# Loading the v tile of an attention unit with one transfer instead of three

## The chip, the cores and the metric

The kernel runs on one core of one Trainium2 chip. The metric is the device time of one execution in microseconds (us). The core has five engines that run their own instruction queues side by side: TensorE (PE; its weight loads are shown apart, as PEld), VectorE (DVE), ScalarE (ACT), GpSimd (POOL) and SyncE (SP). In this kernel SP does no arithmetic; it issues nearly all transfers between HBM and the on-chip memory, in program order, and stops at the first one whose wait isn't met. 16 DMA engines move the data.

## The reference

Linear attention with two softmaxes, and then a token-and-channel mixer on its output. In float32, with batch 8, 8 heads, 576 positions and head size 64:

```python
q_s = softmax(q, axis=-1)                      # over the 64 features
k_s = softmax(k, axis=2)                       # over the 576 positions
kv  = einsum('bhsd,bhse->bhde', k_s, v)        # 64 x 64 per head
x   = einsum('bhsd,bhde->bhse', q_s, kv)       # then laid out as (8, 576, 512)

h   = relu(x.T @ w_tok1) @ w_tok2              # over positions: 576 -> 256 -> 576
u   = x + h.T
out = u + relu(u @ w_ch1) @ w_ch2              # over channels: 512 -> 1536 -> 512
```

## The kernel before

The attention and the token mixing run unit by unit. A unit is one batch and two heads (128 features); there are 32 units, n = 0 to 31. Positions go on the 128 partitions: 576 positions make C = 4 full blocks of 128 and a tail of TL = 64, so that a tile has C1 = 5 blocks. The host lays out the input arrays with that padding; rows 64 to 127 of the tail block repeat the last 64 positions. The matmuls that make `kv` (`stage_kv`, L355) multiply all 5 blocks over all 128 partitions, so what those repeated rows hold must count for nothing there: in the v tile they are zero.

The v tile `v_t` is `[128, 5 blocks, 2 heads, 65]`. Columns 0 to 63 hold v, and column 64 holds ones, which makes the softmax's sum come out of the same matmul. `v_tile` (L60) allocates it once and lets POOL set the ones (L62) and then the whole tail rows, ones column included, to zero (L63). `load_v` (L180) then writes v into the 64-wide parts around the ones column, with three transfers: the 4 full blocks of head 0, those of head 1 (both L184), and the 64 rows of the tail for both heads (L185). As 65 columns lie between one head's part and the next, each contiguous run that the transfer writes is 64 floats, 256 bytes.

The first 8 units (the early ones) use two v tiles in turn, the other 24 units one. `load_v(n + 1)` (or `n + 2` for early units) is issued behind the matmuls of `stage_kv(n)`, and its transfer waits until the last unit in that buffer has been read by them. On the SP queue the v transfers stand between others: `kt_t` (L169) and `q_t` (L161), `k_t` (L174, late units alone), the weight loads `stg` and `stg_w` (L196, L222), the loads and stores that keep sums of weights in HBM (L502, L503, L511, L519), and from 300 us on the `ring` loads (L546), 252 blocks of weights that the channel mixing uses up one after the other.

The early units (until about 80 us) come with the widening and splitting of the weights on DVE and ACT. After that the list `steps` goes over 9 groups of 512 positions and 12 blocks of the hidden channels: `ch1` (L482), or `pair_a` and `pair_b` with `product` (L593), and `ch2` (L642). The late units are put between these steps by the table `todo`. The order on each engine is then set when the program is built, by a planner that simulates the times of all instructions, transfers included:

```python
with tile.TileContext(nc, schedule_with_timeline_sim=True) as tc:
    attn_mixer_kernel(tc, *args, out, dims)
```

Of the kernel before, what the change touches and what calls it, by code (L numbers as in the profile page):

```python
# [15 lines left out]
P = 128  # L16
# [4 lines left out]
def attn_mixer_kernel(ctx: ExitStack, tc: tile.TileContext, q, k, kt, v, wt, out, dims):  # L21
# [3 lines left out]
    nc = tc.nc  # L25
    B, H, S, D, TOK, DM, DCH, wide = dims
# [3 lines left out]
    C = S // P  # L30
    C1 = C + 1
    S0 = C * P
    TL = S - S0
# [26 lines left out]
    def v_tile(pool):  # L60
        t = pool.tile([P, C1, 2, D + 1], F32, name="v_t")
        nc.gpsimd.memset(t[:, :, :, D : D + 1], 1.0)  # L62
        nc.gpsimd.memset(t[TL:P, C, :, :], 0.0)  # L63
        return t

    v_ring = [v_tile(const)]

    ones = const.tile([P, P], F32, name="ones")
# [111 lines left out]
    def load_v(n):  # L180
        if n < NU and n not in v_of:
            t = v_ring[n % 2 if n < NE else 0]
            for h in range(2):
                nc.sync.dma_start(t[:, 0:C, h, 0:D], v[n][:, 0:C, h * D : (h + 1) * D])  # L184
            nc.sync.dma_start(t[0:TL, C, :, 0:D], v[n][0:TL, C, :].rearrange("p (h d) -> p h d", h=2))  # L185
            v_of[n] = t

    def load_weights(i, n=CW, out=None):
# [159 lines left out]
    def stage_kv(u):  # L348
        kx, vt = u["k"], v_of[u["n"]]
        kv = ps_unit()  # L350

        for c in range(C1):
            for h in range(2):
                hs = slice(h * D, (h + 1) * D)
                nc.tensor.matmul(kv[hs, 0 : D + 1], kx[:, c, hs], vt[:, c, h, :], start=(c == 0), stop=(c == C))  # L355

        if u["n"] != NE - 1:
            load_v(u["n"] + 2 if u["n"] < NE else u["n"] + 1)
        rs = sm.tile([P, 1], F32, name="rs")
        nc.vector.tensor_scalar(rs, kv[:, D : D + 1], 1e-9, None, op0=ALU.add)  # L360
        nc.vector.reciprocal(rs, rs)
        kvf = kv_ring[u["n"] % len(kv_ring)]
        for h in range(2):
            hs = slice(h * D, (h + 1) * D)
            nc.scalar.activation(kvf[hs, hs], kv[hs, 0:D], AF.Copy, scale=rs[hs])
        u["kvf"] = kvf
        if u["early"]:
            return
        kvh = wk.tile([P, P], F32R, name="kvh")
        kvl = wk.tile([P, P], F32R, name="kvl")  # L370
        split(kvh, kvl, kvf, nc.vector)
        u["kvh"], u["kvl"] = kvh, kvl
# [176 lines left out]
    rows = {}  # L549
# [161 lines left out]
    w1f = early1.tile([P, C1, TOK], F32, name="w1f")  # L711
    w1t = early1.tile([P, TOK], F32, name="w1t")
    v_ring.append(v_tile(early1))
    kv_ring += [kv_tile(early1, i) for i in range(1, NB)]

# [8 lines left out]
    load_tok1()  # L724
    first = []
    load_v(0)
    begin(1)
    stages[0][0]()
    soft(1)
    stages[0][1]()  # L730
    load_v(1)
    load_tok2()
    conv[:] = [(stg, cv)]
# [168 lines left out]
```

## Time and profile before

| what | value |
|---|---|
| time, median of 3 runs (range) | 813.62 us (811.61 to 817.54) |
| the profiled execution, its own time | 814.48 us |
| its span, first to last instruction | 812.6 us |
| mean granted TensorE clock | 0.998 |
| busy: PE, PEld, DVE, ACT, POOL | 96%, 85%, 74%, 47%, 14% of the span |
| transfers: bytes, mean rate | 147.07 MB, 181 GB/s |

The profile's page gives the busy time of each engine, a strip of 40 slices of the span, the DMA queues, the chain of work that ended last, and groups of instructions by line. A busy PE isn't a PE at its peak, because its matmuls overlap. SPq stands for the queue of SP, PEldq for that of the weight loads; issuing and waiting there aren't counted as busy time of an engine. Further views used below are the table by stretches of time, the waits (who waited for whom), the list of one tile's instructions, and the timeline of one engine.

### The profile page before, as it was taken

What the parts mean: (1) busy time and instruction counts of PE and PEld (TensorE: products, weight loads), DVE (VectorE), ACT (ScalarE), POOL (GpSimd) and SP (SyncE); (2) the same over time, 40 slices, a digit from 0 to 9 for tenths busy, and PEclk for the clock granted to TensorE, in tenths of its full rate; (3) what the DMA queues carried; (4) which work ended last, traced back from release to release, by engine and by line L of the source; (5) the groups of instructions that cost most, each with busy time, mean ns of one, the idle gap of its engine ahead of it and who ended that gap; (6) DMA issues with size and microseconds to landing.
All of it is one profiled execution on the core that took longest, in us unless ns stands there. A gap on an engine that the chain in (4) does not pass through costs nothing.

```text
span 812.6 us, 14046 instructions
## 1 busy us (share of the span) xinstructions
PE 782.8 (96%) x5112; PEld 690.4 (85%) x5112; DVE 605.3 (74%) x1195; ACT 379.9 (47%) x908; POOL 113.8 (14%) x88
## 2 busy tenths in 40 slices
PE   3899999979999999999999999999999999999998
PEld 3688888768878888899999999879999999999996
DVE  7988998789869765987798688877896546436433
ACT  4775533366555654555564455355665522112110
POOL 1000010101212151122212222122122200200000
PEclk9999999999999999999999999999999999999999
DMA  9644632425678643575667656756566445556651
GB/s 300 197 158 146 245 143 92 150 72 188 200 232 283 210 115 98 177 253 175 193 193 243 188 181 186 229 175 191 165 182 209 145 143 179 191 177 205 209 169 52
DMA packets 110852, 147.07 MB, mean 181 GB/s; under 512 B 45760, under 2 KB 57664, under 8 KB 110784
## 3 DMA queue, kind: packets, MB, share of 16 engines
q1 hardware_dynamic: 104448, 134.12, 53.3%
q10 hardware_dynamic: 6336, 12.06, 4.1%
q8 instruction: 41, 0.67, 0.3%
q14 instruction: 27, 0.22, 0.1%
HBM read 122.55 MB, written 23.59 MB: 180 GB/s over the span
## 4 chain that ended last, share of the span: by engine, by line
PE 75%; DVE 11%; DMA 7%; ACT 4%; issue 2%; SPq 1%; POOL 0%; DVEq 0%; ACTq 0%; POOLq 0%
PE ps_o L642 31%; PE ps_h L593 20%; PE ps_h L482 8%; PE ps_h L459 6%; PE ps_h L417 4%; DMA q_t<-in_q 4%; PE ps_h L355 2%; DMA stg<-in_w 1%; ACT q_t L403 1%; PE ps_h L425 1%; DVE q_t L325 1%; DVE q_t L338 1%; PE ps_h L314 1%; DMA k_t<-in_k 1%; DVE st L324 1%
## 5 line engine op out<-in xcount | busy, mean ns | idle before, releaser
L642 PE MATMUL ps_o<-h,c2h 128*128 128x512 f32 x672 | 226.0, 398 | 3.7 <-ACT h L485 3.4
L642 PEld LDWEIGHTS ps_o<-h,c2h 128*128 128x128 f32 x672 | 125.9, 189 | 29.3 <-ACT h L485 4.3
L642 PE MATMUL ps_o<-h,c2l 128*128 128x512 f32 x336 | 132.3, 395 | 0.0
L593 PE MATMUL ps_h<-th,ring 128*128 128x256 f32 x576 | 107.1, 283 | 1.3 <-DVE c L624 1.3
L593 PEld LDWEIGHTS ps_h<-th,ring 128*128 128x128 f32 x576 | 89.7, 191 | 1.5 <-DVE c L624 1.5
L593 PE MATMUL ps_h<-uh,ring 128*128 128x256 f32 x432 | 81.9, 283 | 0.5 <-ACT dg L315 0.5
L593 PE MATMUL ps_h<-tl,ring 128*128 128x256 f32 x288 | 81.4, 283 | 0.0
L593 PEld LDWEIGHTS ps_h<-uh,ring 128*128 128x128 f32 x432 | 70.3, 190 | 5.1 <-ACT dg L315 0.9
L403 ACT COPY q_t<-cv_s 32x160 f32<-32x160 f32 (+1 forms) x232 | 71.9, 310 | 2.8
L316 POOL TENSOR_TENSOR k_t<-k_t,dg 128x640 f32<-128x640 f32 x24 | 40.9, 1704 | 230.5 <-ACT dg L315 215.9
L642 PEld LDWEIGHTS ps_o<-h,c2l 128*128 128x128 f32 x336 | 63.9, 190 | 10.5
L131 POOL TENSOR_TENSOR ql<-q_t,qh 128x640 fp32r<-128x640 f32 x24 | 40.4, 1683 | 182.3 <-ACT qh L130 126.0
L593 PE MATMUL ps_h<-ul,ring 128*128 128x256 f32 x216 | 61.0, 282 | 0.0
L629 ACT ACTIVATE h<-c 128x512 fp32r<-128x512 f32 x48 | 28.9, 625 | 60.2 <-DVE c L624 60.1
L482 PE MATMUL ps_h<-uh,c1h 128*128 128x512 f32 x144 | 56.0, 391 | 0.4 <-ACT c1h L130 0.4
L482 PE MATMUL ps_h<-uh,c1l 128*128 128x512 f32 x144 | 56.2, 390 | 0.0
L482 PE MATMUL ps_h<-ul,c1h 128*128 128x512 f32 x144 | 56.1, 390 | 0.0
L593 PEld LDWEIGHTS ps_h<-tl,ring 128*128 128x128 f32 x288 | 55.2, 192 | 0.0
L466 ACT CAST uh<-ps_h 128x320 fp32r<-128x320 f32 (+4 forms) x76 | 24.8, 336 | 55.7 <-PE ps_h L459 36.5
L334 ACT ACTIVATE q_t<-q_t 128x640 f32<-128x640 f32 x32 | 23.7, 740 | 50.2 <-DVE q_t L325 34.8
L324 DVE TENSOR_REDUCE st<-q_t 128x10 f32<-128x640 f32 x32 | 26.1, 815 | 27.2 <-DMA q_t<-in_q 27.0
L403 DVE COPY q_t<-cv_s 32x160 f32<-32x160 f32 (+1 forms) x152 | 36.7, 241 | 6.8 <-POOL ql L131 5.0
(196 smaller groups left out, 1762.3 us busy)
## 6 DMA issues: line engine op xcount, KB each, us to landing
ring<-w SPq DMA_DIRECT2D x252, 256.0 KB, 3.3
kt_t<-in_kt SPq DMA_DIRECT2D x32, 320.0 KB, 3.3
q_t<-in_q SPq DMA_DIRECT2D x32, 320.0 KB, 3.4
stg_w<-in_w SPq DMA_DIRECT2D x18, 512.0 KB, 6.3
v_t<-in_v SPq DMA_DIRECT2D x64, 128.0 KB, 3.4
k_t<-in_k SPq DMA_DIRECT2D x24, 320.0 KB, 3.8
w<-stg SPq DMA_DIRECT2D x12, 512.0 KB, 3.6
stg<-in_w SPq DMA_DIRECT2D x10, 512.0 KB, 4.8
```

The source lines that it names most:

```text
L131: lo_eng.tensor_tensor(lo, src, f32(hi), op=ALU.subtract)
L316: nc.gpsimd.tensor_tensor(kx, kx, dg.unsqueeze(1).broadcast_to([P, C1, P]), op=ALU.subtract)
L324: nc.vector.tensor_reduce(st[:, 0, :], qt, axis=AX.X, op=ALU.max)
L334: nc.scalar.activation(qc, qc, AF.Exp)
L403: eng(qx[ys, 0:n, xs], turned[xs, 0:n, ys])
L417: nc.tensor.matmul(y[:, 0:TOK], a, w, start=(i == 0), stop=(i == len(mm) - 1))
L459: nc.tensor.matmul(t[:, 0:N], a, w, start=(i == 0), stop=(i == len(mm) - 1))
L466: nc.scalar.copy(uh, src).ins,
L482: nc.tensor.matmul(t, a[:, n, :], w, start=(i == 0), stop=(i == 3 * NJ - 1))
L593: nc.tensor.matmul(t[:, cols], a, b[:, n], start=(i == 0), stop=(i == 5))
L629: nc.scalar.activation(hh, c[:, r], AF.Relu)
L642: m = nc.tensor.matmul(o, a[:, cs], w, start=(first and i == 0), stop=(last and i == 2))
```

## The change

The array of v on the host gets zeros in the rows 64 to 127 of its tail block, where it repeated the last positions. `load_v` moves the whole unit, all 5 blocks, both heads and all 128 partitions, with one transfer. POOL's second memset sets only the ones column of the tail rows to zero, since the transfer now writes the rest.

```diff
@@ v_tile
         nc.gpsimd.memset(t[:, :, :, D : D + 1], 1.0)
-        nc.gpsimd.memset(t[TL:P, C, :, :], 0.0)
+        nc.gpsimd.memset(t[TL:P, C, :, D : D + 1], 0.0)
@@ load_v
             t = v_ring[n % 2 if n < NE else 0]
-            for h in range(2):
-                nc.sync.dma_start(t[:, 0:C, h, 0:D], v[n][:, 0:C, h * D : (h + 1) * D])
-            nc.sync.dma_start(t[0:TL, C, :, 0:D], v[n][0:TL, C, :].rearrange("p (h d) -> p h d", h=2))
+            nc.sync.dma_start(t.rearrange("p c h d -> p (c h) d")[:, :, 0:D], v[n].rearrange("p c (h d) -> p (c h) d", h=2))
@@ kernel, on the host
-    def rows(x):
+    def rows(x, again=None):
         x = x.reshape(nu, 2, s, d)[:, :, twice].reshape(nu, 2, c + 1, P, d)
+        if again is not None:
+            x[:, :, c, tl:] = again
...
-        "in_v": rows(inputs["v"]),
+        "in_v": rows(inputs["v"], 0.0),
```

## The prediction

> **What bounds the kernel now.** I read the page first, then the table by stretches, then the chain of waits, and last SP's timeline around v.
>
> ```profile
> span 812.6 us, 14046 instructions
> PE 782.8 (96%) x5112; PEld 690.4 (85%) x5112; DVE 605.3 (74%) x1195; ACT 379.9 (47%) x908; POOL 113.8 (14%) x88
> q1 hardware_dynamic: 104448, 134.12, 53.3%
> PE 75%; DVE 11%; DMA 7%; ACT 4%; issue 2%; SPq 1%; POOL 0%; DVEq 0%; ACTq 0%; POOLq 0%
> ...
> 0.00:20.00 20.00, 7.38 (x41) 6.04 (x42) 15.88 (x35) 9.57 (x18) 2.16 (x17) 1.00 0.97 301
> 20.00:40.00 20.00, 17.67 (x139) 13.78 (x138) 20.00 (x54) 14.58 (x33) 0.00 (x0) 1.00 0.67 198
> 60.00:80.00 20.00, 19.28 (x151) 17.18 (x150) 17.08 (x30) 12.00 (x31) 0.00 (x0) 1.00 0.43 147
> 160.00:240.00 80.00, 73.42 (x424) 61.72 (x423) 66.88 (x146) 47.32 (x117) 12.47 (x8) 0.98 0.54 171
> 320.00:400.00 80.00, 80.00 (x581) 73.00 (x580) 62.76 (x124) 41.52 (x104) 16.80 (x11) 1.00 0.60 185
> 480.00:560.00 80.00, 77.84 (x551) 69.90 (x550) 66.32 (x131) 43.61 (x115) 17.82 (x10) 1.00 0.65 198
> ```
>
> The fourth row is the chain that ended last, shared out by engine; SP's queue has 1% of it, about 8 us. The table's columns are the stretch, its length, the busy time of PE, PEld, DVE, ACT and POOL, the granted clock, the DMA share and GB/s. PE has work in every moment of 320 to 400, and the other stretches from 240 to 800 look like it, save 480 to 560. A transfer that comes earlier there finds PE busy and gains nothing. PE's idle time is 812.6 - 782.8 = 29.8 us: 12.6 in the first 20 us, 2.3 in the next, 6.6 in 160 to 240, 2.2 in 480 to 560. In 20 to 40 DVE is busy without a break (20.00 of 20). So the change can win only where PE waits and where v's transfers stand in the chain that makes it wait.
>
> **The change part by part.** *SP's queue.* First the prices.
>
> ```profile
> L184 SPq DMA_DIRECT2D v_t<-in_v x64: 368/457/1418, 3.5 to 635.1; - x64
> L185 SPq DMA_DIRECT2D v_t<-in_v x32: 601/602/1838, 5.2 to 635.7; - x32
> L161 SPq DMA_DIRECT2D q_t<-in_q x32: 327/333/596, 1.2 to 607.6; - x32
> ...
> 243.26 0.93 SPq L184 DMA_DIRECT2D v_t<-in_v  x2
> 244.29 0.61 SPq L185 DMA_DIRECT2D v_t<-in_v  x1
> 244.94 0.58 SPq L174 DMA_DIRECT2D k_t<-in_k  x1
> ```
>
> The first three rows give the shortest, middle and longest issue in ns; then come start and length in us on SP's timeline. From v's first issue to k_t's stand 244.94 - 243.26 = 1.68 us, and k_t's own issue takes 0.58 where an undisturbed one takes 0.33. Each issue in such a row is held up by the one before it: the two of L184 take 0.93 together where the shortest takes 0.37, the tail 0.60. The tail has only 64 x 2 = 128 runs of 256 bytes and the halves 128 x 4 = 512 each, and yet what follows the tail is held as long as what follows a half. So the hold goes by transfers rather than by runs. The new transfer has 128 x 10 = 1280 runs, and no row has one like it. Bounds: if the hold goes by transfers, it takes 0.37, a gap of 0.05, and k_t starts at 0.43 instead of 1.68, a gain of 1.25. If it goes by runs, the hold behind a half (0.60 - 0.37 = 0.23 over the free issue) becomes 1280/512 as much, 0.58, and the gain is 1.25 - 0.35 = 0.9. The worst end is the longest issue in the rows, 1.84: k_t then comes 0.2 us later than now. I take 1.2, since the tail's row is the nearest. The waits that stand ahead of v's first issue (the matmuls L355 must be done with the buffer) stay.
>
> *Bytes.* The zero rows add 32 KB per unit, 32 x 32,768 = 1.05 MB, and 32 x 128 = 4,096 packets. At 53.3% of 16 engines x 812.6 us for q1's 104,448 packets, one takes 66 ns; 4,096 of them are 17 us of 16 engines at most, 0.5 us per unit. I cost that at nothing, because the late units move while the 16 engines are 54 to 65% busy (the column of shares above) and v has a whole unit's time to land (64 issues of L184 from 3.5 to 635.1 are 32 units of 20 us); if that cover were gone it would be 0.5 us on what stands behind v, and that is the part of 1.2 that could be lost.
>
> [...]
>
> *Place 1, the early units.*
>
> ```profile
> 38.17 0.92 SPq L184 DMA_DIRECT2D v_t<-in_v  x2
> 40.99 0.86 SPq L222 DMA_DIRECT2D stg_w<-in_w  x2
> 42.69 0.33 SPq L161 DMA_DIRECT2D q_t<-in_q  x1
> ...
> 42.69 7.06 DMA q_t<-in_q
> 65.65 0.16 SPq L185
> 65.86 0.58 SPq L222
> 66.50 4.80 DMA stg_w<-in_w
> ...
> 64.19 0.93 SPq L184 DMA_DIRECT2D v_t<-in_v  x2
> ...
> DVE st L324 <- DMA q_t<-in_q: 1.9, 2, 1.3
> DVE cv_w L232 <- DMA stg_w<-in_w: 1.6, 1, 1.6
> PE ps_o L459 <- DVE hl L433: 0.9, 1, 0.9
> ```
>
> At 64.19 v of the last early unit is issued, and the weight loads L222 stand behind it at 65.86. They are on the chain; DVE waits 1.6 us for them, and PE 0.9 for DVE at 80 us. With one transfer L222 starts at about 64.65, and those waits shrink by 1.2. Late next is ACT, which widens these weights (L233); I take the 1.2 whole, since DVE's wait is longer than it. At 38.17 it is the same in small: stg_w goes out 1.2 earlier, and q_t, whose 7.06 us are mostly a wait behind stg_w's two blocks, lands earlier. DVE waited 1.3 us for it. q_t's own issue at 42.69 hangs on PE and doesn't move, so I take half, 0.6. What this wins lies before 80 us, where PE's unbroken work begins, and moves all of it. Together 1.8, bounds 0 and 2.9 (1.3 and 1.6).
>
> *Place 2, the first late units.* At 186 the tail's issue was held 1.84 us, and k_t, with the sums of weights behind it, is on the chain:
>
> ```profile
> 185.84 0.40 SPq L184
> 186.34 1.84 SPq L185
> 188.23 3.53 DMA k_t<-in_k
> 192.63 5.71 DMA stg<-whole
> ...
> PE ps_h L459 <- ACT qth L130: 1.5, 1, 1.5
> PE ps_o L642 <- ACT h L485: 3.4, 2, 3.3
> ```
>
> PE waits 6.6 us between 160 and 240, but 3.3 and 1.5 of that (the last two rows, at 165.8 and 176.5) lie ahead of this place and hang on weight loads and on ACT, so that 1.8 is left. The chain gets from here to PE over many steps of DVE and ACT; I take 0.8, bounds 0 and 1.8.
>
> *Place 3, 500 to 560.*
>
> ```profile
> 501.56 0.41 SPq L184
> 502.06 0.60 SPq L185
> 502.71 2.94 DMA k_t<-in_k
> ...
> PE ps_h L593 <- DVE c L624: 1.3, 1, 1.3
> ```
>
> Again k_t stands behind v, and the chain ends in PE's wait of 1.3 at 536. PE's 2.2 of idle time is the upper bound; I take 0.7, bounds 0 and 1.2.
>
> *PE's queue.* The matmuls of `stage_kv` had three landings to wait for and now have one.
>
> ```profile
> L355 PEldq EVENT_SEMAPHORE  x32: 51/51/1206, 12.3 to 651.0; - x32
> ...
> L63 POOL MEMSET v_t<- x2: 203/203/203, 1.6 to 2.7; 64x130 f32 x2
> ```
>
> There is one separate wait of 51 ns per unit, 1.6 us over 32. Some of these may go, and PE is the bound there; a wait for k's values remains. I take 0.4, bounds 0 and 1.6. The memsets of 0.2 us on POOL stand at 1.6 and 2.7 us, ahead of v's first issue at 3.55, and what they save is hidden by the transfers already on SP: nothing.
>
> Sum: 1.8 + 0.8 + 0.7 + 0.4 = 3.7 us, bounds 0 and 2.9 + 1.8 + 1.2 + 1.6 = 7.5. Against the profiled execution's own 814.48 (its span of 812.6 and 1.9 around it) that gives 810.8; against the median of 813.62, 809.9. I say 810.
>
> **The rivals.** *Nothing reaches the end.* The waits of PE at the three places hang on DVE and ACT with work of their own, which then is late instead; or the new transfer's 1280 runs hold SP as long as the three did. For it: the chain has 1% on SP's queue. The time is 812 to 815.5.
>
> *Slower, by the planner's order.* 64 transfers fewer, and others of another length, change the times that the planner simulates, and with them the order on DVE and ACT. The place is 140 to 240 and 480 to 560, where DVE is 82 to 84% busy (66.88 and 66.32 of 80) and PE already waits. The price of one bad place is a row above: 3.3 us, where PE waits for ACT's h, which stands behind a widening that waits for its load. Two such more, 6.6, and the 3.7 not won: 814.48 + 6.6 = 821. It decides from the point at which one instruction that PE needs next is put behind a wait of more than about 1 us. Against it: most of PE's work lies from 240 on, where nothing waits for long.
>
> *Better, by the same means.* A luckier order removes the 3.3 and the 1.5 in 160 to 240 as well: 810.8 - 4.8 = 806; with the upper bounds of the rest (7.5 instead of 3.7) 802.
>
> *The change doesn't do what it says.* If the one transfer were cut into as many pieces when it is built, SP would show them, and the time would be the first rival's.
>
> **How the numbers follow.** The forecast, 806.5 to 812, has 0.52; nothing won, 812 to 815.5, 0.27 (the last rival with it); slower by the order, 815.5 to 824, 0.13; better by the order, below 806.5, 0.08. One per cent of this kernel, about what a measurement can tell from no change, is 8.1 us: below 805.5 lies most of the last case, 0.07; above 821.8 about half of the third, 0.06; the rest, 0.87, is no change that can be told. The range leaves out the outer parts of the two order cases: 804 to 819.
>
> **What would show each step.** SP's timeline should show one L183 issue of 0.37 to 0.6 us in each unit and the next transfer starting 0.4 to 0.7 us after v's, not 1.68. At 64 us the weight loads should go out 1.2 us earlier relative to v, and DVE's wait for stg_w should be below 0.6. In 160 to 240 and 480 to 560 PE should be busy 74 and 78.5 of 80. The separate waits of L355 should be fewer than 32. q1 should have 4,096 packets more. An issue of v above 1.5 us, or k_t held as long, would make the step on SP wrong; PE idle in places where it had none, with the same instructions in another order, would show the planner's rival.

## The result, and the profile after

| | median (us) | range (us) | executions |
|---|---|---|---|
| before | 815.23 | 811.61 to 817.54 | 18 |
| changed | 810.05 | 808.51 to 812.15 | 18 |

The ratio is 0.994, 95% interval [0.9929, 0.9951]: 5.2 us less. The 3 runs that front the document had a median of 813.62; with 18 it is 815.23. The profiled execution of the changed kernel took 811.71 us itself, with a span of 809.9; that of before took 814.48. Single executions of one kernel lie up to 6 us apart, so traces are used below to say where something happens, and medians to say what it is worth. Line numbers from 185 on are 2 lower than before.

The page of the changed kernel, with the rows that answer to those of before (span, busy time, SP's transfers, the chain by engine):

```profile
span 809.9 us, 13915 instructions
PE 782.0 (97%) x5112; PEld 691.0 (85%) x5112; DVE 608.1 (75%) x1195; ACT 380.1 (47%) x908; POOL 111.6 (14%) x88
q1 hardware_dynamic: 107520, 135.16, 53.7%
PE 73%; DVE 16%; DMA 6%; ACT 2%; issue 2%; SPq 0%; POOL 0%; ACTq 0%; DVEq 0%; POOLq 0%
```

SP's queue has left the chain (1% before), and q1's bytes grew by 1.04 MB, as forecast (1.05). The packets grew by 3,072, not 4,096: 107,520 - 104,448. 64 transfers fewer take 1,024 packets with them, 16 each, which the forecast had left out; a run below with 96 transfers more has 1,536 packets more, again 16 each.

The table by stretches of the changed kernel (the columns as before: PE, PEld, DVE, ACT, POOL, granted clock, DMA share, GB/s):

```profile
20.00:40.00 20.00, 16.39 (x108) 12.89 (x107) 19.68 (x49) 13.17 (x29) 0.00 (x0) 0.91 0.68 188
60.00:80.00 20.00, 20.00 (x147) 17.40 (x147) 18.57 (x34) 13.42 (x35) 0.00 (x0) 1.00 0.52 166
160.00:240.00 80.00, 76.11 (x445) 64.16 (x441) 70.46 (x150) 47.55 (x120) 13.46 (x8) 0.98 0.54 176
480.00:560.00 80.00, 78.63 (x567) 71.61 (x566) 67.26 (x133) 44.28 (x117) 15.71 (x11) 1.00 0.64 198
```

PE gained 2.7 us in 160 to 240 (73.42 before) and 0.8 in 480 to 560 (77.84), and 60 to 80 is full now (19.28). In 20 to 40 it lost 1.3, at a clock of 0.91. DVE does 3.6 us more in 160 to 240 than before, with the same 1195 instructions in all: work stands elsewhere. So I compared the two orders, place by place on each engine (v's own transfers count as one; both orders are written out in the kernels of experiment 2, and the times are those in the trace of before):

```
engine   instructions   in another place   last difference
PE       4,648          428                265 us
DVE      1,195          342                294 us
ACT        951          157                270 us
```

On SP it is 32 of 448. The planner has ordered these engines anew up to about 294 us and left the rest as it was. The prediction held that as a risk; it is now the first rival to its own steps.

Next the single steps. The list of the v tile, with shortest, middle and longest issue in ns, and the landing of the transfers:

```profile
L183 SPq DMA_DIRECT2D v_t<-in_v x32: 539/551/648, 3.6 to 632.1; - x32
L63 POOL MEMSET v_t<- x2: 97/97/97, 1.6 to 2.6; 64x2 f32 x2
DMA to landing us min/median/max: 3.4/4.3/8.8
```

And SP's timeline of the changed kernel in one late unit:

```profile
285.50 0.56 SPq L183 DMA_DIRECT2D v_t<-in_v  x1
286.11 0.75 SPq L174 DMA_DIRECT2D k_t<-in_k  x1
```

v's issue takes 0.55 us and k_t's starts 0.6 us behind v's, where it was 1.68: 1.08 earlier. But k_t's own issue now takes 0.75 instead of 0.58. Counted from v's first issue, the whole of v lands after 4.3 us, and with three transfers it took 4.5 (medians of the 18 late units from 235 to 632 us): one transfer of 1280 runs lands hardly earlier than three.

PE's waits between 82 and 340 us in the changed kernel (who waited for whom, us in all, times, longest):

```profile
PE ps_o L640 <- ACT h L483: 4.3, 3, 2.5
PE ps_h L457 <- ACT hh L430: 0.7, 2, 0.4
PE ps_h L457 <- DVE hl L431: 0.3, 1, 0.3
```

These are 5.3 us; the same view of before sums to 7.1. The wait of 1.5 for qth at 176.5 is gone. The longest wait for h went from 3.3 to 2.5, but there are three of them now, and their sum rose from 3.4 to 4.3. Two more traces of the changed kernel, taken with the experiments, have 5.2 and 3.6 in the place of 5.3. This is the one with 3.6:

```profile
PE ps_o L640 <- ACT h L483: 3.2, 3, 2.5
PE ps_h L457 <- ACT hh L430: 0.4, 1, 0.4
```

Differences of 1 to 2 us between single traces can therefore be chance.

### The profile page after: what moved, and what is told of

It is laid out like the page before. It is cut to its first block, busy times and chain, and to the rows that moved or that the text cites. A ratio compares the mean times of both kernels' runs of the same rounds, so it can differ in the third digit from the quotient of the medians.

```text
span 809.9 us, 13915 instructions
## 1 busy us (share of the span) xinstructions
PE 782.0 (97%) x5112; PEld 691.0 (85%) x5112; DVE 608.1 (75%) x1195; ACT 380.1 (47%) x908; POOL 111.6 (14%) x88
## 3 DMA queue, kind: packets, MB, share of 16 engines
q1 hardware_dynamic: 107520, 135.16, 53.7%
## 4 chain that ended last, share of the span: by engine, by line
PE 73%; DVE 16%; DMA 6%; ACT 2%; issue 2%; SPq 0%; POOL 0%; ACTq 0%; DVEq 0%; POOLq 0%
PE ps_o L640 29%; PE ps_h L591 21%; PE ps_h L480 6%; PE ps_h L457 6%; PE ps_h L415 4%; DMA q_t<-in_q 4%; PE ps_h L353 2%; DVE q_t L401 1%; PE ps_h L423 1%; DVE st L322 1%; PE ps_o L457 1%; DVE st L333 1%; DVE q_t L323 1%; DMA whole<-cv_s 1%; DVE q_t L336 1%
## 5 line engine op out<-in xcount | busy, mean ns | idle before, releaser
L640 PEld LDWEIGHTS ps_o<-h,c2l 128*128 128x128 f32 x336 | 63.6, 189 | 10.5
L591 PEld LDWEIGHTS ps_h<-ul,ring 128*128 128x128 f32 x216 | 41.0, 190 | 0.1
```

What stands on the lines that cost most here:

```text
L591: nc.tensor.matmul(t[:, cols], a, b[:, n], start=(i == 0), stop=(i == 5))
L640: m = nc.tensor.matmul(o, a[:, cs], w, start=(first and i == 0), stop=(last and i == 2))
```

## The experiments

Two theories. S is the prediction's: fewer transfers hold SP's queue for less time, so k_t and the weight loads behind v come earlier, and PE waits less. Its rival is that the planner's other order does it, whatever the transfers do.

**1. One transfer in a part of the units, and steps between three and one.** The planner orders each of these kernels by itself. The diffs are against the kernel before and show v's transfers alone: with one transfer the zeros on the host belong to it as in the change, and the memset of POOL stays the large one in all four.

Late units (n >= NE) with one transfer:

```diff
-            for h in range(2):
+            for h in range(0 if n >= NE else 2):
                 nc.sync.dma_start(t[:, 0:C, h, 0:D], ...)
-            nc.sync.dma_start(t[0:TL, C, :, 0:D], ...)
+            nc.sync.dma_start(*((t.rearrange("p c h d -> p (c h) d")[:, :, 0:D], ...) if n >= NE else (t[0:TL, C, :, 0:D], ...)))
```

> The early 8 units keep three transfers, the 24 late ones get one. Theory S (SP's queue: in each late unit k_t and what stands behind it go out about 1.1 us after v instead of 1.7): the stretch from 285 us to the end, where the order on every engine is that of before, gets about 1.5 us shorter, as in the changed kernel, and the whole kernel 3 to 5 us (809.5 to 812 where before is 814 to 815). Theory O (the planner's new order up to 285 us makes the difference): this kernel has an order of its own, so the time up to 285 us moves by up to 3 us either way, and the end alone gains nothing.

The reverse, early units with one transfer and late ones with three:

```diff
-            for h in range(2):
+            for h in range(0 if n < NE else 2):
```

> The early 8 units get one transfer, the 24 late ones keep three. Theory S: from 285 us to the end nothing changes against before (within 0.3 us); the first 80 us give at most 1 us, since there the changed kernel's trace was not ahead. Time 814 to 815 where before is 815. Theory O: the order up to 285 us is like that of the changed kernel in its first 80 us, and most of the changed kernel's gain (3 us or more) is here too.

Two transfers: the full blocks of both heads in one, the tail of 64 rows as before.

```diff
-            for h in range(2):
-                nc.sync.dma_start(t[:, 0:C, h, 0:D], v[n][:, 0:C, h * D : (h + 1) * D])
+            nc.sync.dma_start(t.rearrange("p c h d -> p (c h) d")[:, 0:2 * C, 0:D], v[n][:, 0:C, :].rearrange("p c (h d) -> p (c h) d", h=2))
             nc.sync.dma_start(t[0:TL, C, :, 0:D], ...)
```

> Two transfers in every unit: the 4 full blocks of both heads in one, the tail's 64 rows in another; no zero rows are moved. Theory S: k_t starts about 1.15 us after v instead of 1.68 before and 0.60 in the changed kernel, so that half of the gain from 285 us to the end is there, about 0.7 us of 1.5. Theory O: the order is that of before up to about 155 us, and differs in few places until 285 us; the time is within 1 us of before.

Three transfers, the tail with its zero rows: the bytes of the change without its saving of transfers.

```diff
-            nc.sync.dma_start(t[0:TL, C, :, 0:D], v[n][0:TL, C, :].rearrange("p (h d) -> p h d", h=2))
+            nc.sync.dma_start(t[:, C, :, 0:D], v[n][:, C, :].rearrange("p (h d) -> p h d", h=2))
```

> Three transfers as before, but the tail's moves all 128 rows, the 64 zero rows too, and the second memset is small as in the changed kernel: the bytes of the changed kernel, the count of before. Theory S: from 285 us to the end no gain and no loss (within 0.3 us), the whole time that of before or up to 1 us longer. Theory O: the planner's order up to 285 us is again another one, so the time moves by up to 3 us although the queue has the same transfers; a gain of 3 us or more would speak for the order.

(The small memset that this expectation names isn't in the kernel that ran; POOL sets the whole tail rows as before.)

Measured, beside 816.15 us of before (35 executions; 12 of each other kernel):

| kernel | median (us) | ratio, 95% interval |
|---|---|---|
| late units one | 813.09 | 0.9965 [0.9948, 0.9982] |
| early units one | 813.32 | 0.9969 [0.9952, 0.9986] |
| two | 814.75 | 0.9983 [0.9964, 1.0001] |
| three with zero rows | 814.54 | 0.9984 [0.9966, 1.0003] |

Either half of the units gives about half of the gain. But four planner's orders are mixed into these numbers, and the last row, which saves no transfer, comes out as well as the row with two. These runs alone can't part the theories. Two expectations of S fell. The early units were to give at most 1 us and gave 2.5 by the ratio (interval 1.1 to 3.9). And the late part was to be shorter by 1.5 us. From the first product matmul (L593) to the end of the span the traces show 477.0 us for before, 475.5 for the changed kernel, 476.9 for late units one, and 475.7, 475.7 and 476.2 for the other three; this doesn't follow the late units' transfers.

**2. Transfers and order apart.** Edges without a semaphore tie the instructions of each engine into the order of the one kernel or of the other, so that the planner has no choice left (the lists of the orders are not printed here). In the trace of one transfer in the order of before, PE's 5,112 matmuls stand in the same order as before. Each of the first three kernels differs from the one whose order it has in the transfers alone, and in the memset and the zeros on the host that belong to them.

```diff
     ch2(*pend[0][1:], in_turn=True)
     out_end(*pend[0][:2], True)
+    pin(tc, list(v_ins.values()))
...
+def pin(tc, v_ins):      # for each engine, in the order of the donor
+            ...
+            tc.add_manual_dep(i, last.name, info, reason="pin")   # NoSync
```

One transfer, order of before:

> The changed kernel's single transfer, with the order of every engine pinned to that of before (issue order alone, no waits added; SP's list has the one transfer where the first of the three stood). Theory S (fewer transfers on SP's queue shorten the waits themselves): most of the changed kernel's gain is here, 3 us or more of its 5. Theory O (the gain is the planner's order): within 1 us of before. If the two share it, 2 to 3 us.

Three transfers, order of the changed kernel:

> The three transfers of before, with the order of every engine pinned to that of the changed kernel (the three stand where the one stood). Theory S: within 1 us of before, since the queue is as long as before. Theory O: most of the gain, 3 us or more. If the two share it, 2 to 3 us, and with the run of one transfer in the old order they add up to the changed kernel's gain.

Two transfers, order of before:

> Two transfers per unit (the full blocks of both heads, and the tail's 64 rows), with the order pinned to that of before. Theory S: between before and the single transfer in the old order, about half of that gain, 1 to 2 us. Theory O: within 1 us of before.

The changed kernel as it is, beside them:

> The changed kernel once more, as it is, beside the others of this call on the same chip: 0.994 of before, about 5 us faster, under either theory; its trace is a second one to read beside the first.

Measured, beside 817.13 us of before (23 executions; 12 of each kernel in the order of before, 6 in the new one):

| transfers | order of before | new order |
|---|---|---|
| three | 1 (817.13 us) | 0.9939 [0.9922, 0.9956] (812.63) |
| two | 0.9972 [0.9957, 0.9986] (814.06) | not run |
| one | 0.9968 [0.9952, 0.9985] (814.53) | 0.9928 [0.9913, 0.9943] (811.28) |

Both count. In us by the ratios: in the old order one transfer wins 0.32%, 2.6. The new order with three transfers wins 0.61%, 5.0, and one transfer on top of it 0.11% more, 0.9, which these intervals don't tell from nothing. Taken the other way round, the order adds 0.40%, 3.3, to one transfer. So the order is worth 3.3 to 5.0 of the 5.9 us here, and the transfers 0.9 to 2.6: most of the result is the planner's order. The two single gains, 2.6 and 5.0, are more than the 5.9 of both together. Whether they overlap isn't shown: the two kernels between the corners are tied, the corners are not, and no kernel was run tied to its own order, so what the ties themselves do to the time isn't known. That two transfers do as well as one speaks against a gain that grows with every transfer saved.

PE's waits from 82 to 340 us with three transfers in the new order:

```profile
PE ps_o L642 <- ACT h L485: 3.1, 3, 2.5
PE ps_h L425 <- ACT ys L419: 1.4, 1, 1.4
PE ps_h L459 <- ACT hh L432: 1.0, 1, 1.0
PE ps_h L459 <- DVE hl L433: 1.0, 2, 0.5
PE ps_o L642 <- DVE h L486: 0.2, 1, 0.2
```

The 3.3 for h is 2.5 in longest wait here too, and the 1.5 for qth is gone: that is the order's doing. 6.7 us in all remain, against 5.3, 5.2 and 3.6 in the three traces with one transfer. The 0.9 at 80 us, which the prediction gave to the weight loads, is gone here as well, with three transfers.

**3. More transfers, and v behind k_t.** If S holds in either order, doubling the transfers must cost, and k_t ahead of v must win.

```diff
             for h in range(2):
-                nc.sync.dma_start(t[:, 0:C, h, 0:D], v[n][:, 0:C, h * D : (h + 1) * D])
-            nc.sync.dma_start(t[0:TL, C, :, 0:D], ...)
+                nc.sync.dma_start(t[:, 0:2, h, 0:D], v[n][:, 0:2, h * D : (h + 1) * D])
+                nc.sync.dma_start(t[:, 2:C, h, 0:D], v[n][:, 2:C, h * D : (h + 1) * D])
+            for h in range(2):
+                nc.sync.dma_start(t[0:TL, C, h, 0:D], ...)
```

> Six v transfers per unit instead of three (each head's full blocks in two, the tail in one per head), the order of every engine as in the kernel before. Theory S (the fixed-order gain of 2.6 us is the hold of each v transfer on SP's queue): three more transfers hold k_t and the weight loads 3 x 0.42 = 1.3 us longer, and the time grows by 2 to 4 us (ratio 1.003 to 1.005). Rival, N (with the order fixed, what counts is something that two, one and three transfers share or a difference of the pairs of runs): within 1 us of the kernel before, ratio 0.999 to 1.001.

> The same six transfers, the order of every engine as in the changed kernel. Theory H (the new order hides most of what v holds on SP's queue, since one transfer there won only 0.9 us over three): at most 1.5 us above three transfers in that order, ratio to the kernel before 0.994 to 0.996. Theory S without that cover: 2 to 4 us above, ratio 0.9965 to 0.999.

The changed kernel in its own order, except that on SP the v of units 9 and 12 to 30 and the k_t behind it change places:

```diff
 # the order for SP that pin() sets, at the v of these units
-    v_t, k_t
+    k_t, v_t
```

> The changed kernel with its order, but in 20 late units v is issued behind k_t instead of ahead of it. k_t then goes out 0.6 us earlier and none of v's bytes stand ahead of its own. If k_t's landing is still on the path (Theory S): 1 to 2 us less than the changed kernel of the same call. If the new order hides it (Theory H): within 0.7 us of it.

> The changed kernel as it is, for comparison with the three others of this call: ratio 0.992 to 0.995.

Measured, beside 815.39 us of before (17 executions; 12 with six transfers in the new order, 6 of each other):

| kernel | median (us) | ratio, 95% interval |
|---|---|---|
| six, order of before | 823.75 | 1.0106 [1.0077, 1.0135] |
| six, new order | 817.62 | 1.0025 [1.0007, 1.0043] |
| one, new order, v behind k_t | 808.86 | 0.9909 [0.9888, 0.9930] |
| changed, as it is | 810.12 | 0.9931 [0.9905, 0.9958] |

By the ratios, three transfers more cost 8.6 us in the old order, and 7.0 in the new one, where six give 1.0025 and three gave 0.9939 beside the earlier runs of before. Both are well above the 2 to 4 that S expected, and the theory that the new order hides what v holds fell. So v's transfers do reach the end; only the step from three to one is small. SP's timeline of six transfers in the new order shows the hold:

```profile
462.54 0.38 SPq L184 DMA_DIRECT2D v_t<-in_v  x1
463.01 0.42 SPq L185 DMA_DIRECT2D v_t<-in_v  x1
463.49 0.46 SPq L184 DMA_DIRECT2D v_t<-in_v  x1
464.04 0.42 SPq L185 DMA_DIRECT2D v_t<-in_v  x1
464.55 1.11 SPq L187 DMA_DIRECT2D v_t<-in_v  x2
465.72 0.58 SPq L174 DMA_DIRECT2D k_t<-in_k  x1
```

k_t starts 3.18 us behind v's first issue. PE's waits from 82 to 340 us in that kernel name who is late:

```profile
PE ps_o L644 <- ACT h L487: 3.8, 3, 2.5
PE ps_o L644 <- DVE h L488: 1.9, 1, 1.9
PE ps_h L461 <- DVE hl L435: 1.8, 3, 0.9
PE ps_h L427 <- ACT ys L421: 1.5, 1, 1.5
PE ps_h L461 <- ACT hh L434: 0.7, 2, 0.5
```

9.7 us, against 6.7 with three and 5.3, 5.2 and 3.6 with one. Most of what is new is a wait for DVE.

Where the time goes can be read more closely. With three and with six transfers PE's order is the same, so each matmul can be set beside itself. It starts so much later with six (us, worked out from the traces, half-speed stretches included):

| time with three transfers (us) | 80 | 200 | 280 | 500 | end |
|---|---|---|---|---|---|
| order of before | 4.0 | 3.8 | 9.5 | 9.5 | 8.5 |
| new order | 1.5 | 3.0 | 5.0 | 5.0 | 4.7 |

All is lost before 280 us. After that the late units have six transfers each and lose nothing. What grows and shrinks with the times is DVE's wait for `q_t`, which stands behind v in several units. From 160 to 300 us, in the order of before with three and with six transfers:

```profile
DVE st L324 <- DMA q_t<-in_q: 9.3, 5, 2.8
DVE st L326 <- DMA q_t<-in_q: 15.4, 6, 5.2
```

With two and one it is 6.6 and 6.9. In the new order it is 10.5 with six, 7.2 with three and 6.7 to 7.6 in the three traces with one. That this wait makes the time, by way of DVE, fits, but no run tests it alone.

Why does the step from three to one win so little? A part of the answer is in the landings behind v. I took the landing of k_t itself, counted from the first issue of the pair of v and k_t, in the 18 late units from 235 to 632 us (medians, worked out from the issues and landings of each unit):

| transfers | order | k_t's issue starts (us) | k_t has landed (us) |
|---|---|---|---|
| six | before / new | 3.20 / 3.18 | 6.50 / 6.41 |
| three | before / new | 1.68 / 1.68 | 5.36 / 5.52 |
| two | before | 1.14 | 5.04 |
| one | before / new | 0.60 / 0.60 | 5.08 / 5.25 |
| one, v behind k_t | new | 0.00 | 4.17 |

From six to three the columns shrink by 1.5 and about 1.0. From three to one the issue comes 1.08 earlier and the landing only 0.3. From two to one nothing is left, as in the times. With k_t ahead of v its landing comes 1.1 earlier again, and v's comes 1.0 later (5.3 instead of 4.3). From three transfers to one, whichever of the two is issued first has landed after 4.2 to 4.6 us, and the other after 5.0 to 5.5. The author's estimate from these landings is that what stands behind v waits for v's bytes, and that saving an issue hardly shortens that; no run shows this wait by itself. And these landings alone don't give the time: the 18 units lie mostly in the part in which even six transfers lose nothing, and the landing of k_t that comes 1.1 earlier again won 1.3 us by the medians, not told from nothing.

SP's timeline of the kernel with v behind k_t:

```profile
455.13 0.33 SPq L174 DMA_DIRECT2D k_t<-in_k  x1
455.52 0.55 SPq L185 DMA_DIRECT2D v_t<-in_v  x1
```

Its waits of PE from 480 to 560 us, and then those of the changed kernel:

```profile
PE ps_h L593 <- DVE c L624: 0.9, 1, 0.9
```

```profile
PE ps_h L591 <- DVE c L622: 1.3, 1, 1.3
```

The wait at 536 is down to 0.9, as it should be if it hangs on k_t's landing. But six transfers, with which k_t lands 1.0 later, have 1.3 there in the new order and less than before in the old one:

```profile
PE ps_h L595 <- DVE c L626: 1.1, 1, 1.1
```

So that this wait hangs on k_t's landing isn't shown. This kernel's ratio to before is the lowest of all, and its median lies 1.3 us under the changed kernel beside it, but the intervals of the two overlap, and this kernel is tied where that one isn't.

## Why the prediction was right or wrong, step by step

The time, 810 forecast and 810.05 measured, was right. That it was met so closely is luck: the forecast took 3.7 us off a median of 813.62, and measured were 5.2 off one of 815.23. Of the forecast 3.7 us the transfers alone gave 2.6 in the old order and 0.9, not told from nothing, in the new one. The order, which the sum had at nothing, gave the most.

**SP's queue: the issue right, its size a little off, the step from issue to landing wrong.** The new issue takes 0.55 (0.37 taken, "0.37 to 0.6" in the list of what would show it), and k_t starts 0.60 behind v, within the list's 0.4 to 0.7: a gain of 1.08, between "1.2, since the tail's row is the nearest" and the 0.9 of the bound by runs. The failed step is that 1.2 us earlier at the issue were taken as 1.2 us earlier at the landing. For k_t they were 0.3. A row of the list of the v tile before could have said it: each of the three landed a middle of 3.4 us after its own issue, twice the 1.68 that the issues took.

**Place 1, 1.8 forecast: not shown.** (The v at 64.19 is that of unit 8, the first late one; the prediction calls it that of the last early unit.) In the order of before with one transfer, SP's timeline at the weight loads is this:

```profile
65.23 0.54 SPq L185 DMA_DIRECT2D v_t<-in_v  x1
65.87 2.23 SPq L222 DMA_DIRECT2D stg_w<-in_w  x4
```

L222 follows 0.64 us after v instead of 1.67 (64.19 to 65.86 before), 1.03 earlier where 1.2 was forecast. But DVE, which waits for them, in that kernel and then in before (start, length, and in brackets the wait ahead):

```profile
74.16 0.70 DVE L232 TENSOR_SCALAR cv_w<-stg_w 128x1024 uint32<-128x1024 uint32 x1 [2.73 <-DMA stg_w<-in_w]
```

```profile
72.11 0.69 DVE L232 TENSOR_SCALAR cv_w<-stg_w 128x1024 uint32<-128x1024 uint32 x1 [1.58 <-DMA stg_w<-in_w]
```

Counted from v's issue the weights reach DVE 8.93 us later, and before 7.92. The wait grew to 2.7 instead of shrinking below 0.6. In the changed kernel it did shrink, to 0.4, but with three transfers in the same order it is 0.3: the sign came true through the order, which issues two of these four loads ahead of that v. The other half of the place, q_t, came true in the order of before, where DVE's wait for it until 82 us went from 1.9 to 0.2 us. In the changed kernel it is 3.0, and 2.8 with three transfers in that order: there the order made it longer. None of it reached PE by then: its waits from 20 to 82 us sum to 3.5 in before and to 3.5 with one transfer in the same order. And at the start, which the prediction held for covered, what stands behind the single transfer is held long (the changed kernel on SP):

```profile
3.63 0.65 SPq L183 DMA_DIRECT2D v_t<-in_v  x1
4.32 3.68 SPq L169 DMA_DIRECT2D kt_t<-in_kt  x1
8.04 0.55 SPq L183 DMA_DIRECT2D v_t<-in_v  x1
8.63 2.93 SPq L194 DMA_DIRECT2D stg_w<-in_w  x1
```

The first L222 (L220 here) goes out at 13.03 here and at 12.54 in before; the order of the loads ahead of it differs too.

**Place 2, 0.8 forecast: the place is right, its size isn't shown.** Most of what six transfers cost is lost between 160 and 280 us. PE's waits from 82 to 340 us go 9.7 and 6.7 with six and three transfers in the new order, 5.3, 5.2 and 3.6 with one, and 3.2 with v behind k_t. In the old order they are 13.0 with six and 7.1 with three, but 8.2 with one. Single traces carry no better than that; where the 2.6 us of one transfer in the old order lie isn't shown.

**Place 3, 0.7 forecast: too large.** The wait at 536 stays at 1.3 in all three traces of the changed kernel. PE's 78.63 of 80 looks like the forecast 78.5 and comes from other, smaller waits. That k_t's landing moves this wait is supported by the one run that put k_t ahead and contradicted by the two with six transfers.

**PE's queue, 0.4 forecast: nothing.** The changed kernel still has the separate waits, one fewer than before:

```profile
L353 PEldq EVENT_SEMAPHORE  x31: 51/51/549, 13.2 to 648.3; - x31
```

**The rivals.** The prediction gave the planner's order 0.13 for harm and 0.08 for help. It helped, by 3.3 to 5.0 us; the traces show a part of it. It did some of what "a luckier order" describes: the wait of 1.5 went, the longest for h fell from 3.3 to 2.5 (the sum of them did not fall), and the 0.9 at 80 us went, which the prediction had counted as a gain of the transfers. What was missed is that a new order comes with the change of the transfers as long as the planner is free, and that here it was worth more than they were. "Nothing reaches the end" is wrong for six transfers and, by the interval of 1.2 to 3.9 us, for one in the order of before; in the new order the step from three to one isn't told from nothing.

## What to carry to other kernels

For an issue saved on a queue, count what the landing of the next transfer gains, not what its issue gains (here 0.3 us, not 1.08), and count it only in stretches where the path waits for what lands. Where a planner sets the order from simulated times, every edit of a transfer is two changes; tie the order down and run the two apart before a gain is put down to the edit, and run a kernel tied to its own order beside them. Doubling a cost that seems too small to measure shows whether its place matters.

## What the runs showed of the hardware

Stretches of TensorE at half speed, a granted clock of 0.50, come and go from one execution to the next. The time from 30 to 35 us in the changed kernel, which has such a stretch from 30.88 to 34.30, and in its trace taken with experiment 3, which has none there:

```profile
30.00:35.00 5.00, 4.45 (x32) 3.77 (x33) 5.00 (x13) 4.80 (x12) 0.00 (x0) 0.66 0.57 170
```

```profile
30.00:35.00 5.00, 4.65 (x41) 3.65 (x42) 3.84 (x11) 4.60 (x13) 0.00 (x0) 1.00 0.81 274
```

The 3.4 us at 0.50 are an estimated 1.7 lost. The execution without it had a span of 806.9 us, that with it 809.9. Between 20 and 40 us PE had waited 1.9 and 1.7 us in the one with the stretch, 0.4 and 1.0 in the other. The two stretches of the changed kernel that end within the span (from 30.88 and 167.42 us) and the one of before (165.42) last 3.4 us each; a third of the changed kernel starts at 809.12, when PE has done its work. In the 3.41 us ahead of them PE was busy for 1.50, 0.89, 0.52 and 0.23 us. But in before it was busy for 1.70 of 3.41 us from 28.00 to 31.41, and the clock was 1.00 until 40.

The mean granted clock was 0.9957 in 35 executions of before and 0.9977 in the 18 of the changed kernel; the difference, 0.002 of 812 us, is an estimated 1.6 us of the 5.2 won. It goes with the order rather than with the step from three transfers to one: 0.9951 with one transfer in the order of before, 0.9970 with three in the new one. With six in the new one it was 0.9953. That the shorter waits of PE bring it is the author's estimate, not shown.

The issue of a transfer with 1280 runs of 256 bytes took 0.55 us, of one with 512 runs 0.37 at the least, and of one with 128 runs, behind another, 0.60. So 2.5 times the runs took 1.5 times as long to issue. What stood behind v's transfer took longer too: k_t's issue 0.75 behind one v of 1280 runs and 0.33 ahead of it, and at the start, where the 16 DMA engines were 93% busy (0 to 20 us), an issue of kt_t behind v took 3.68 us.
